# First product of an MLP: the 64-row remainder of its contraction as pairs of 64-row matmuls

## The chip, the cores and the metric

The kernel runs on one core of a Trainium2 chip. The metric is the device time of one execution in microseconds; the time before is the median of three executions.

## What is computed

Eight batches of 4224 rows of 192 columns pass through a dynamic convolution, a two-dimensional Fourier mixing and an MLP:

```
w = softmax(weight_gen)                      # 8 heads, 7 taps
x = causal convolution of x_in with w, per head
X = real(fft(fft(x, axis=1), axis=2))
u = x + X
un = (u - mean(u)) / sqrt(var(u) + 1e-6)
ch = maximum(un @ w_ch1, 0.0) @ w_ch2        # 192 -> 768 -> 192
out = u + ch
```

## The kernel before, in words

A batch's 4224 rows are laid out as 33 rows on each of 128 partitions. Four of those rows make a group (a tile of 128 partitions, 4 rows, 192 columns); a batch has eight groups of four and one of a single row, so there are 72 groups, 64 of them full. Per batch the stages are: `conv` (taps and sums, mostly on VectorE and GpSimd, with the first Fourier factor on TensorE, result through DRAM), `transform` (second factor, TensorE and ScalarE), `mix` (last factor and the addition to u), `norm` and `mlp`. Each stage is a Python generator. `run` (from L617) advances, of all the generators, the one whose due time is earliest; the due times are set at the end (from L685). So the program text interleaves the stages of neighbouring batches. The tile framework then orders the instructions of every engine by its own simulated times, and adds the semaphores; the order that an engine gets is not that of the text.

`norm` (L504) computes statistics on ScalarE, scales u to `un` (f32) and splits it in two fp16 parts: `hl` holds the rounded part (ScalarE, L538) and the rest (`lo`, on GpSimd, for the first few groups on VectorE, L540 and L542). Per row that is 384 columns: 192 rounded and 192 rest. One DMA transpose (L545, SP's queue) turns them into `ht`: per row three blocks of 128 partitions. Block 0 holds columns 0 to 127 rounded, block 2 the rest of those columns, block 1 the remaining 64 columns: rounded on partitions 0–63 and their rest on partitions 64–127.

`mlp(n)` (L550) runs the first product of group n and the second product of group n−1 side by side. The weights are split the same way: `w1h0`, `w1l0` (128 rows of W1, rounded and rest) and `w1h1`, `w1l1` (the last 64 rows, held twice, on partitions 0–63 and 64–127). For each of the six chunks c of 128 hidden columns, five matmuls (L570) add up in one PSUM bank `ph` (three buffers), all of 128 rows and 4 × 128 = 512 columns:

```
terms = ((w1h0, 0), (w1l0, 0), (w1h0, 2), (w1h1, 1), (w1l1, 1))
for i, (wt, blk) in enumerate(terms):
    nc.tensor.matmul(ph[:, 0:T], lhsT=wt[:, cs_], rhs=ht[:, 0:T, blk], ...)
```

ScalarE then takes the ReLU out of the bank to fp16 (`hh`, L580; f32 in the first nine groups, L576), and VectorE the rest of it (`hlo`, L581). The second product (L597) takes hh and hlo of one row and one chunk as the stationary operand and 192 columns of W2 as the moving one: three matmuls per row and chunk (one f32 matmul in the first nine groups), added up in `po` (two banks, two rows each). When all chunks are through, VectorE adds both banks to u (L604) and SP's queue writes it out (L607).

In the sections below, a matmul of 64 rows is called a half.

Of the kernel before, what the change touches and what calls it, by code (L numbers as in the profile page):

```python
# [19 lines left out]
P = 128  # L20
# [18 lines left out]
F32_GROUPS = 9  # L39
# [48 lines left out]
def tile_dynconv_fnet_mlp(  # L88
# [12 lines left out]
    nc = tc.nc  # L101
    B, D = x.shape[0], x.shape[3]
# [3 lines left out]
    NH = DFF // P  # L106
    w1 = w1.bitcast(I32).rearrange("r (c t) -> r c t", t=2)
    w2 = w2.bitcast(I32).rearrange("r (c t) -> r c t", t=2)
    NG = 9

    cpool = ctx.enter_context(tc.tile_pool(name="cpool", bufs=1))
    sb = ctx.enter_context(tc.tile_pool(name="sb", bufs=2))
# [3 lines left out]
    def pst(tag, bufs, shape, dt, name):  # L116
        return ps.tile(shape, dt, tag=tag, name=name, bufs=bufs)
# [14 lines left out]
    w1h0 = cpool.tile([P, DFF], F16, name="w1h0")  # L132
    w1l0 = cpool.tile([P, DFF], F16, name="w1l0")
    w1h1 = cpool.tile([P, DFF], F16, name="w1h1")
    w1l1 = cpool.tile([P, DFF], F16, name="w1l1")
    w2h = cpool.tile([P, NH, D], F16, name="w2h")
    w2l = cpool.tile([P, NH, D], F16, name="w2l")
    w2f = cpool.tile([P, NH, D], F32, name="w2f")
    isc = cpool.tile([P, 1], F32, name="isc")
# [364 lines left out]
    def norm(b, g):  # L504

        T = min(4, N2 - 4 * g)
        u = uv = us[b, g]
        st = sb.tile([P, 4, 2], F32, tag="st", name=f"st_{b}_{g}", bufs=2)
        rs = sb.tile([P, 3, 4], F32, tag="rs", name=f"rs_{b}_{g}", bufs=2)
        junk = sb.tile([P, D], F16, tag="junk", name=f"junk_{b}_{g}", bufs=2)  # L510
        un = sb.tile([P, 4, D], F32, tag="un", name=f"un_{b}_{g}", bufs=1)
        quick = NG * b + g < QUICK or (b == 1 and g < 2)
        if quick:
            bn = sb.tile([P, 4, 6], F32, tag="bn", name=f"bn_{b}_{g}", bufs=2)
            for t in range(T):
                nc.vector.bn_stats(out=bn[:, t, :], in_=uv[:, t, :])
                last_bn[b, g] = nc.vector.bn_aggr(out=st[:, t, :], in_=bn[:, t, :])
            nc.scalar.activation(rs[:, 0, 0:T], st[:, 0:T, 1], AF.Sqrt, bias=eps_t)
            neg = -1.0
        else:  # L520
            for t in range(T):
                nc.scalar.activation(junk, uv[:, t, :], AF.Identity, accum_out=st[:, t, 0:1])  # L522
            neg = -1.0 / D
            nc.scalar.mul(rs[:, 2, 0:T], st[:, 0:T, 0], neg)
            for t in range(T):
                nc.scalar.activation(junk, uv[:, t, :], AF.Square, bias=rs[:, 2, t:t + 1],  # L526
                                     accum_out=st[:, t, 1:2])
            nc.scalar.activation(rs[:, 0, 0:T], st[:, 0:T, 1], AF.Sqrt, bias=eps_t, scale=1.0 / D)
        nc.vector.reciprocal(out=rs[:, 0, 0:T], in_=rs[:, 0, 0:T])
        for t in range(T):  # L530
            nc.vector.tensor_scalar(out=rs[:, 1, t:t + 1], in0=st[:, t, 0:1], scalar1=rs[:, 0, t:t + 1],  # L531
                                    scalar2=neg, op0=ALU.mult, op1=ALU.mult)
        for t in range(T):
            nc.scalar.activation(un[:, t, :], uv[:, t, :], AF.Identity,  # L534
                                 bias=rs[:, 1, t:t + 1], scale=rs[:, 0, t:t + 1])
        yield 0.5
        hl = sb.tile([P, 4, 2 * D], F16, tag="hl", name=f"hl_{b}_{g}", bufs=2)
        nc.scalar.copy(hl[:, 0:T, 0:D], un[:, 0:T, :])  # L538
        lo_eng = nc.vector if quick else nc.gpsimd
        lo_eng.tensor_tensor(out=hl[:, 0:T, 2 * P:3 * P], in0=un[:, 0:T, 0:P],  # L540
                                in1=hl[:, 0:T, 0:P], op=ALU.subtract)
        last_lo[NG * b + g] = lo_eng.tensor_tensor(out=hl[:, 0:T, D:2 * P], in0=un[:, 0:T, P:D],  # L542
                                in1=hl[:, 0:T, P:D], op=ALU.subtract)
        ht = sb.tile([P, 4, 3, P], F16, tag="ht", name=f"ht_{b}_{g}", bufs=3)
        nc.sync.dma_start(ht[:, 0:T].rearrange("p t q m -> p (t q) m"),  # L545
                          hl[:, 0:T, :].rearrange("p t d -> p (t d)"), transpose=True)
        state[b, g] = (us.pop((b, g)), ht)
        yield 2.0

    def mlp(n):  # L550

        now = last = None
        if n < total:
            b, g = divmod(n, NG)
            T = min(4, N2 - 4 * g)
            u, ht = state.pop((b, g))
            now = (b, g, u, [], [])
        if n - 1 in pending:
            last = pending.pop(n - 1)
            lb, lg, lu, hh, hlo = last  # L560
            LT = min(4, N2 - 4 * lg)
            LJ = (LT + 1) // 2
            po = [pst("po", 2, [P, 2, D], F32, f"po_{lb}_{lg}_{jj}") for jj in range(LJ)]
        for c in range(NH):
            if now:
                ph = pst("ph", 3, [P, 4, P], F32, f"ph_{b}_{g}_{c}")
                cs_ = slice(c * P, (c + 1) * P)
                terms = ((w1h0, 0), (w1l0, 0), (w1h0, 2), (w1h1, 1), (w1l1, 1))
                for i, (wt, blk) in enumerate(terms):
                    last_ph[n] = nc.tensor.matmul(ph[:, 0:T], lhsT=wt[:, cs_], rhs=ht[:, 0:T, blk],  # L570
                                                  start=(i == 0), stop=(i == len(terms) - 1))
                    if i < len(terms) - 1:
                        yield (c + 0.1 * (i + 1)) / NH
                if NG * b + g < F32_GROUPS:
                    a, l = sb.tile([P, 4, P], F32, tag="hh", name=f"hh_{b}_{g}_{c}", bufs=10), None
                    nc.scalar.activation(a[:, 0:T], ph[:, 0:T], AF.Relu)  # L576
                else:
                    al = sb.tile([P, 2, 4, P], F16, tag="hh", name=f"hh_{b}_{g}_{c}", bufs=10)
                    a, l = al[:, 0], al[:, 1]
                    nc.scalar.activation(a[:, 0:T], ph[:, 0:T], AF.Relu)  # L580
                    nc.vector.scalar_tensor_tensor(out=l[:, 0:T], in0=ph[:, 0:T], scalar=0.0,  # L581
                                                   in1=a[:, 0:T], op0=ALU.max, op1=ALU.subtract)
                now[3].append(a)
                now[4].append(l)
                yield (c + 0.5) / NH
            if last:
                s, half = divmod(c, NH // 2)
                for c2 in (2 * half, 2 * half + 1):
                    for jj in range(LJ):
                        t = 2 * jj + s  # L590
                        if t >= LT:
                            continue
                        terms = ((hh[c2], w2f),) if NG * lb + lg < F32_GROUPS else (
                            (hh[c2], w2h), (hh[c2], w2l), (hlo[c2], w2h))
                        nt = len(terms)
                        for i, (hx, wx) in enumerate(terms):
                            nc.tensor.matmul(po[jj][:, s, :], lhsT=hx[:, t], rhs=wx[:, c2, :],  # L597
                                             start=(c2 == 0 and i == 0), stop=(c2 == NH - 1 and i == nt - 1))
                            yield (c + 0.5 + 0.25 * (c2 % 2) + 0.25 * (nt * jj + i + 1) / (nt * LJ)) / NH
                if c == NH - 1:  # L600
                    for jj in range(LJ):
                        m = min(2, LT - 2 * jj)
                        lt = lu[:, 2 * jj:2 * jj + m]
                        nc.vector.scalar_tensor_tensor(out=lt, in0=po[jj][:, 0:m],  # L604
                                                       scalar=scales[0][:, 1:2] if NG * lb + lg < F32_GROUPS else isc, in1=lt,
                                                       op0=ALU.mult, op1=ALU.add)
                    nc.sync.dma_start(out[lb, :, 4 * lg:4 * lg + LT, :], lu[:, 0:LT])  # L607
        yield 1.0
        if now:
            pending[n] = now  # L610
# [30 lines left out]
    last_word, last_split, last_lo, last_bn, last_ph, scales = [], [], {}, {}, {}, []  # L641
# [17 lines left out]
    for g in range(QUICK):  # L659
        add(0.0, 1.0, behind((last_word if g else last_split)[-1].ins, mix(0, g)))  # L660
        run()
        add(0.0, 1.0, norm(0, g))
        run()
        queue(last_bn[0, g].ins, (prep_w2, g))
# [74 lines left out]
```

## Time and profile before

| what | value |
|---|---|
| median of three executions | 1191.4 us (1191.09 to 1192.69) |
| the profiled execution's own time | 1194.52 us |
| its span in the trace | 1192.7 us |
| mean granted TensorE clock | 0.963 |
| TensorE busy with matmuls | 1095.0 us |
| VectorE, GpSimd, ScalarE busy | 1027.1, 867.8, 779.2 us |
| first-product matmuls of 512 columns | 1920 |
| second-product matmuls, fp16 | 4158 |

In the profile, PE is TensorE's matmuls and PEld its weight loads; DVE is VectorE, ACT ScalarE, POOL GpSimd, SP the queue that issues the DMAs. A row of a timeline has the start, the time that the merged instructions took, the engine and line, the operation, the tiles written and read, the shape and the count. Matmuls are pipelined: a recorded one overlaps the next, so what one costs in a row of many is the distance of the starts, not its duration.

### The profile page before, as it was taken

The numbers are of one execution on the slowest core, as the hardware profiler recorded it, in microseconds if no ns is written. First come the engines' busy times: TensorE is split into PE (matmuls) and PEld (weight loads), VectorE is DVE, ScalarE is ACT, GpSimd is POOL, SyncE is SP. The second block draws the span as 40 slices with busy tenths as digits, with TensorE's granted clock in tenths as the row PEclk, the third lists the DMA queues.
The fourth block names the chain that finished last, engine by engine and source line by source line (L and its number), as shares of the span: only waits on it lengthen the run. The fifth ranks groups of instructions, "written<-read, shape, count | busy, mean of one in ns | idle before, by whom it ended". The sixth has DMA issues, their size and how long they took to land. (4 is left out here: it accounts for less than half of the span.)

```text
span 1192.7 us, 23723 instructions
## 1 busy us (share of the span) xinstructions
PE 1095.0 (92%) x8382; PEld 827.0 (69%) x8382; DVE 1027.1 (86%) x2041; ACT 779.2 (65%) x2353; POOL 867.8 (73%) x686
## 2 busy tenths in 40 slices
PE   4775599899899979998999999899989999999998
PEld 2444377678667857687677777678667876877677
DVE  7999998789999999899999999799998997367533
ACT  1015695254597598757895789657885799589732
POOL 3869579839896999699978999599958997002100
PEclk9896599999999989999999999899999999999999
DMA  8235233731348144733474247413543124412311
GB/s 305 84 98 163 40 60 109 192 89 47 99 127 206 50 123 102 191 87 88 112 198 110 61 114 208 125 48 110 147 121 92 54 58 102 111 45 71 75 50 44
DMA packets 156504, 128.73 MB, mean 108 GB/s; under 512 B 108571, under 2 KB 133088, under 8 KB 156384
## 3 DMA queue, kind: packets, MB, share of 16 engines
q1 hardware_dynamic: 156384, 127.21, 39.4%
q8 instruction: 66, 1.08, 0.4%
q14 instruction: 54, 0.44, 0.1%
HBM read 61.46 MB, written 39.37 MB: 85 GB/s over the span
## 5 line engine op out<-in xcount | busy, mean ns | idle before, releaser
L399 POOL TENSOR_TENSOR u<-u,pr 128x768 f32<-128x768 f32 (+1 forms) x395 | 655.3, 1679 | 69.5 <-DVE pr L390 62.6
L570 PE MATMUL ph<-ht,w1h 128*128 128x512 f16 (+1 forms) x1296 | 401.2, 366 | 20.1 <-DMA ht<-hl 8.8
L597 PE MATMUL po<-w2h,hh 128*128 128x192 f16 x2772 | 395.1, 247 | 6.4 <-DVE u L604 6.0
L597 PEld LDWEIGHTS <-hh 128*128 128x128 f16 x4158 | 355.0, 98 | 65.6 <-issue 7.8
L390 DVE TENSOR_TENSOR pr<-x_sb,wp 128x768 f32<-128x768 f32 (+1 forms) x420 | 358.0, 878 | 21.3 <-POOL u L399 16.8
L597 PE MATMUL po<-w2l,hh 128*128 128x192 f16 x1386 | 337.1, 247 | 0.0
L581 DVE SCALAR_TENSOR_TENSOR hh<-ph,hh 128x512 f16<-128x512 f32 (+1 forms) x378 | 238.7, 640 | 98.1 <-ACT hh L580 96.8
L570 PE MATMUL ph<-ht,w1l 128*128 128x512 f16 (+1 forms) x864 | 312.6, 365 | 0.0
L580 ACT ACTIVATE hh<-ph 128x512 f16<-128x512 f32 (+1 forms) x378 | 207.8, 555 | 136.6 <-PE ph L570 135.7
L540 POOL TENSOR_TENSOR hl<-un,hl 128x512 f16<-128x512 f32 (+1 forms) x67 | 71.9, 1073 | 175.3 <-ACT hl L538 129.4
L570 PEld LDWEIGHTS <-w1h 128*128 128x128 f16 x1296 | 127.2, 100 | 101.6 <-issue 6.1
L534 ACT ACTIVATE un<-u,rs 128x192 f32<-128x192 f32 x264 | 125.6, 537 | 19.8 <-DVE rs L531 12.2
L570 PEld LDWEIGHTS <-w1l 128*128 128x128 f16 x864 | 85.3, 99 | 73.2 <-issue 22.1
L526 ACT ACTIVATE junk<-u,rs 128x192 f16<-128x192 f32 x244 | 110.4, 453 | 3.5
L522 ACT ACTIVATE junk<-u 128x192 f16<-128x192 f32 x244 | 87.8, 360 | 16.6 <-DVE u L496 12.1
L486 PE MATMUL eo<-cs_sb,pq 97*128 97x97 f32 x544 | 79.8, 282 | 17.8 <-DVE u L496 13.3
L486 PEld LDWEIGHTS eo<-cs_sb,pq 97*128 97x128 f32 x544 | 73.8, 198 | 24.4 <-issue 13.1
L461 ACT COPY pq<-pp 97x204 f32<-97x204 f32 (+1 forms) x96 | 46.4, 483 | 60.3 <-PE pp L457 59.4
L597 PE MATMUL po<-w2f,hh 128*128 128x192 f32 x396 | 74.3, 337 | 3.5 <-DVE u L604 3.5
L597 PEld LDWEIGHTS po<-w2f,hh 128*128 128x128 f32 x396 | 68.3, 197 | 9.2 <-DVE u L604 5.2
L604 DVE SCALAR_TENSOR_TENSOR u<-po,isc,u 128x384 f32<-128x384 f32 (+1 forms) x119 | 68.0, 597 | 7.7 <-PE po L597 7.2
L395 PE MATMUL pa<-pr,ident 128*128 128x384 f32 x140 | 54.6, 540 | 20.5 <-DVE pr L390 17.8
(101 smaller groups left out, 1309.7 us busy)
## 6 DMA issues: line engine op xcount, KB each, us to landing
out_dram<-u SPq DMA_DIRECT2D x64, 384.0 KB
x_sb<-in_x_dram SPq DMA_DIRECT2D x48, 384.0 KB
g<-g_d SPq DMA_DIRECT2D x40, 336.0 KB
x_sb<-in_x_dram SPq DMA_DIRECT2D x8, 864.0 KB
g_d<-gt SPq DMA_DIRECT2D x32, 195.0 KB
g_d<-gt SPq DMA_DIRECT2D x32, 189.0 KB
w<-in_weight_gen_dram SPq DMA_DIRECT2D x6, 924.0 KB
x_sb<-in_x_dram SPq DMA_DIRECT2D x8, 672.0 KB
```

Of the source, the lines that this page charges most:

```text
L390: last_product[b] = nc.vector.tensor_tensor(out=dst, in0=rows, in1=wk, op=ALU.mult)
L399: adder.tensor_tensor(out=u, in0=u, in1=pr, op=ALU.add)
L486: nc.tensor.matmul(eo[:, e, j, :], lhsT=pq[0:DH, e, r, r:r + P], rhs=cs_sb[:, e, :], start=True, stop=True)
L522: nc.scalar.activation(junk, uv[:, t, :], AF.Identity, accum_out=st[:, t, 0:1])
L526: nc.scalar.activation(junk, uv[:, t, :], AF.Square, bias=rs[:, 2, t:t + 1], accum_out=st[:, t, 1:2])
L534: nc.scalar.activation(un[:, t, :], uv[:, t, :], AF.Identity, bias=rs[:, 1, t:t + 1], scale=rs[:, 0, t:t + 1])
L540: lo_eng.tensor_tensor(out=hl[:, 0:T, 2 * P:3 * P], in0=un[:, 0:T, 0:P], in1=hl[:, 0:T, 0:P], op=ALU.subtract)
L570: last_ph[n] = nc.tensor.matmul(ph[:, 0:T], lhsT=wt[:, cs_], rhs=ht[:, 0:T, blk], start=(i == 0), stop=(i == len(terms) - 1))
L580: nc.scalar.activation(a[:, 0:T], ph[:, 0:T], AF.Relu)
L581: nc.vector.scalar_tensor_tensor(out=l[:, 0:T], in0=ph[:, 0:T], scalar=0.0, in1=a[:, 0:T], op0=ALU.max, op1=ALU.subtract)
L597: nc.tensor.matmul(po[jj][:, s, :], lhsT=hx[:, t], rhs=wx[:, c2, :], start=(c2 == 0 and i == 0), stop=(c2 == NH - 1 and i == nt - 1))
L604: nc.vector.scalar_tensor_tensor(out=lt, in0=po[jj][:, 0:m], scalar=scales[0][:, 1:2] if NG * lb + lg < F32_GROUPS else isc, in1=lt, op0=A ...
```

## The change

For full groups (T = 4) the first product is cut differently. Chunks are taken in pairs, and a bank `ph` no longer holds four rows of one chunk, but two rows of both chunks of the pair: the pair's first bank holds rows 0 and 1, its second one rows 2 and 3. The terms on the first 128 columns (L595) are now six matmuls of 256 columns per bank. The 64-column remainders (L605) are matmuls of 64 rows: `norm` lays the transposed remainder out so that partitions 0–63 of blocks 8 to 11 belong to rows 0 and 1 and partitions 64–127 to rows 2 and 3, and each term is issued twice, once on each half of the partitions, each into its own bank. Three terms × two chunks × two halves make twelve per pair. ReLU and its rest (`keep`) stay one instruction per bank at the old shape. In the second product the index of `hh` changes accordingly, and the loop runs row by row through all chunks, so that the first two rows are finished and added to u halfway (L634). In `norm` the rounding copy becomes two (L547, L548), of 128 and 64 columns per row.

```diff
-        nc.scalar.copy(hl[:, 0:T, 0:D], un[:, 0:T, :])
...
+        if T == 4:
+            flat = hl.rearrange("p t d -> p (t d)")
+            hi0, lo0 = [flat[:, o:o + 4 * P].rearrange("p (t d) -> p t d", t=4) for o in (0, 4 * P)]
+            hi1, lo1 = [flat[:, o:o + 2 * P].rearrange("p (a s d) -> p s a d", a=2, s=2) for o in (8 * P, 10 * P)]
+            un0, un1 = un[:, :, 0:P], un[:, :, P:D].rearrange("p (s a) d -> p s a d", s=2)
...
+        nc.scalar.copy(hi0, un0)
+        nc.scalar.copy(hi1, un1)
+        lo_eng.tensor_tensor(out=lo0, in0=un0, in1=hi0, op=ALU.subtract)
+        last_lo[NG * b + g] = lo_eng.tensor_tensor(out=lo1, in0=un1, in1=hi1, op=ALU.subtract)
...
+            if now and T == 4:
+                j = c % 2
                 ph = pst("ph", 3, [P, 4, P], F32, f"ph_{b}_{g}_{c}")
+                ph2 = [ph] if j == 0 else [ph2[0], ph]
+                pair = (c - j, c - j + 1)
+                for c1 in pair:
+                    co = 2 * (c1 % 2)
+                    for i, (wt, blk) in enumerate(((w1h0, 0), (w1l0, 0), (w1h0, 4))):
+                        last_ph[n] = nc.tensor.matmul(ph[:, co:co + 2], lhsT=wt[:, c1 * P:(c1 + 1) * P],
+                                                      rhs=ht[:, blk + 2 * j:blk + 2 * j + 2],
+                                                      start=(co == 0 and i == 0), stop=False)
+                        yield (c + 0.06 * (3 * (c1 % 2) + i + 1)) / NH
+                if j == 1:
+                    for c1 in pair:
+                        co = 2 * (c1 % 2)
+                        for i, (wt, blk) in enumerate(((w1h1, 8), (w1l1, 8), (w1h1, 10))):
+                            for q in range(2):
+                                h = slice(64 * q, 64 * q + 64)
+                                last_ph[n] = nc.tensor.matmul(ph2[q][:, co:co + 2], lhsT=wt[h, c1 * P:(c1 + 1) * P],
+                                                              rhs=ht[h, blk:blk + 2], start=False,
+                                                              stop=(c1 == c and i == 2))
+                    for q in range(2):
+                        keep(ph2[q], 4)
+                yield (c + 0.5) / NH
...
+                for k in range(per * c, per * (c + 1)):
+                    t, c2 = divmod(k, NH)
+                    i2, t2 = (2 * (c2 // 2) + t // 2, 2 * (c2 % 2) + t % 2) if LT == 4 else (c2, t)
```

What this makes of the order on TensorE, at two places. A name such as ph_5_0_2_10033 is the bank of batch 5, group 0, chunk 2 and a running number; in the change, the bank of an even chunk is the first of its pair and gets the halves on partitions 0–63, that of the odd chunk behind it is the second and gets those on partitions 64–127.

TensorE before, batch 5, group 0, chunk 2, from its second matmul to the second products behind it:

```order
L570 LDWEIGHTS w1l0_82
L570 MATMUL ph_5_0_2_10033<-ht_5_0_9665,w1l0_82 128x512
L570 LDWEIGHTS w1h0_81
L570 MATMUL ph_5_0_2_10033<-ht_5_0_9665,w1h0_81 128x512
L570 LDWEIGHTS w1h1_83
L570 MATMUL ph_5_0_2_10033<-ht_5_0_9665,w1h1_83 128x512
L570 LDWEIGHTS w1l1_84
L570 MATMUL ph_5_0_2_10033<-ht_5_0_9665,w1l1_84 128x512
L597 LDWEIGHTS hh_4_8_5_9946
L597 MATMUL po_4_8_0_9970<-w2h_85,hh_4_8_5_9946 128x192
```

TensorE with the change, the same group, from the fifth of the six halves of the pair's first bank (chunk 2) to the first full matmul of its second (chunk 3):

```order
L605 LDWEIGHTS w1l1_84
L605 MATMUL ph_5_0_2_11768<-ht_5_0_11362,w1l1_84 128x256
L605 LDWEIGHTS w1h1_83
L605 MATMUL ph_5_0_2_11768<-ht_5_0_11362,w1h1_83 128x256
L418 MATMUL pg_6_4_11868<-sm_6_4_11865,f1_sb_67 128x192 x2
L629 LDWEIGHTS hh_4_8_5_11674
L629 MATMUL po_4_8_0_11697<-w2h_85,hh_4_8_5_11674 128x192
L595 LDWEIGHTS w1h0_81
L595 MATMUL ph_5_0_3_11783<-ht_5_0_11362,w1h0_81 128x256
```

All six halves of the first bank have moved up behind its full matmuls; the six on the other partitions stand behind the full matmuls of chunk 3, with other work between.

TensorE with the change, batch 2, group 5, chunks 0 and 1, where the halves begin:

```order
L595 MATMUL ph_2_5_1_6300<-ht_2_5_5830,w1h0_81 128x256
L605 LDWEIGHTS w1h1_83
L605 MATMUL ph_2_5_0_6244<-ht_2_5_5830,w1h1_83 128x256
L605 LDWEIGHTS w1h1_83
L605 MATMUL ph_2_5_1_6300<-ht_2_5_5830,w1h1_83 128x256
L605 LDWEIGHTS w1l1_84
L605 MATMUL ph_2_5_0_6244<-ht_2_5_5830,w1l1_84 128x256
L605 LDWEIGHTS w1l1_84
L605 MATMUL ph_2_5_1_6300<-ht_2_5_5830,w1l1_84 128x256
```

Here the halves alternate between the two banks, as the code is written. Over the whole program there are 2304 full matmuls (L595) and 2304 halves (L605) of 256 columns; a half has one on the other partitions as its neighbour in 433 disjoint pairs, and 1438 stand without a partner. Runs of halves begin 347 times and end 347 times.

More of the change, by code (lines that the diff above doesn't have):

```diff
@@ L537, in norm @@
         hl = sb.tile([P, 4, 2 * D], F16, tag="hl", name=f"hl_{b}_{g}", bufs=2)
-        nc.scalar.copy(hl[:, 0:T, 0:D], un[:, 0:T, :])
         lo_eng = nc.vector if quick else nc.gpsimd
[L540 to L546, printed above, removed]
+        if T == 4:
[3 more added lines that the diff above has]
+            un0, un1 = un[:, :, 0:P], un[:, :, P:D].rearrange("p (s a) d -> p s a d", s=2)
+        else:
+            hi0, hi1, lo1, lo0 = hl[:, 0:T, 0:P], hl[:, 0:T, P:D], hl[:, 0:T, D:2 * P], hl[:, 0:T, 2 * P:3 * P]
+            un0, un1 = un[:, 0:T, 0:P], un[:, 0:T, P:D]
+        nc.scalar.copy(hi0, un0)
+        nc.scalar.copy(hi1, un1)
+        lo_eng.tensor_tensor(out=lo0, in0=un0, in1=hi0, op=ALU.subtract)
+        last_lo[NG * b + g] = lo_eng.tensor_tensor(out=lo1, in0=un1, in1=hi1, op=ALU.subtract)
+        ht = sb.tile([P, 12, P], F16, tag="ht", name=f"ht_{b}_{g}", bufs=3)
+        nc.sync.dma_start(ht[:, 0:3 * T], hl[:, 0:T, :].rearrange("p t d -> p (t d)"), transpose=True)
         state[b, g] = (us.pop((b, g)), ht)
@@ L563, in mlp, with keep @@
             po = [pst("po", 2, [P, 2, D], F32, f"po_{lb}_{lg}_{jj}") for jj in range(LJ)]
+        def keep(ph, w):
+            nm = f"hh_{b}_{g}_{len(now[3])}"
+            if NG * b + g < F32_GROUPS:
+                a, l = sb.tile([P, 4, P], F32, tag="hh", name=nm, bufs=10), None
+                nc.scalar.activation(a[:, 0:w], ph[:, 0:w], AF.Relu)
+            else:
+                al = sb.tile([P, 2, 4, P], F16, tag="hh", name=nm, bufs=10)
+                a, l = al[:, 0], al[:, 1]
+                nc.scalar.activation(a[:, 0:w], ph[:, 0:w], AF.Relu)
+                nc.vector.scalar_tensor_tensor(out=l[:, 0:w], in0=ph[:, 0:w], scalar=0.0,
+                                               in1=a[:, 0:w], op0=ALU.max, op1=ALU.subtract)
+            now[3].append(a)
+            now[4].append(l)
@@ L564, in mlp @@
         for c in range(NH):
-            if now:
+            cs_ = slice(c * P, (c + 1) * P)
+            if now and T == 4:
+                j = c % 2
                 ph = pst("ph", 3, [P, 4, P], F32, f"ph_{b}_{g}_{c}")
-                cs_ = slice(c * P, (c + 1) * P)
+                ph2 = [ph] if j == 0 else [ph2[0], ph]
[19 more added lines that the diff above has]
+                yield (c + 0.5) / NH
+            elif now:
+                ph = pst("ph", 3, [P, 4, P], F32, f"ph_{b}_{g}_{c}")
@@ L568, in mlp @@
                 terms = ((w1h0, 0), (w1l0, 0), (w1h0, 2), (w1h1, 1), (w1l1, 1))
                 for i, (wt, blk) in enumerate(terms):
-                    last_ph[n] = nc.tensor.matmul(ph[:, 0:T], lhsT=wt[:, cs_], rhs=ht[:, 0:T, blk],
+                    last_ph[n] = nc.tensor.matmul(ph[:, 0:T], lhsT=wt[:, cs_], rhs=ht[:, blk:blk + T],
                                                   start=(i == 0), stop=(i == len(terms) - 1))
@@ L573, in mlp @@
                         yield (c + 0.1 * (i + 1)) / NH
[L574 to L582, printed above, removed]
@@ L583, in mlp @@
-                now[3].append(a)
-                now[4].append(l)
+                keep(ph, T)
                 yield (c + 0.5) / NH
             if last:
[L587 to L599, printed above, removed]
@@ L600, in mlp @@
-                if c == NH - 1:
[L601 to L606, printed above, removed]
+                f32 = NG * lb + lg < F32_GROUPS
@@ new lines, in mlp @@
+                per = LT
+                for k in range(per * c, per * (c + 1)):
+                    t, c2 = divmod(k, NH)
+                    i2, t2 = (2 * (c2 // 2) + t // 2, 2 * (c2 % 2) + t % 2) if LT == 4 else (c2, t)
+                    terms = ((hh[i2], w2f),) if f32 else ((hh[i2], w2h), (hh[i2], w2l), (hlo[i2], w2h))
+                    for i, (hx, wx) in enumerate(terms):
+                        nc.tensor.matmul(po[t // 2][:, t % 2, :], lhsT=hx[:, t2], rhs=wx[:, c2, :],
+                                         start=(c2 == 0 and i == 0), stop=(c2 == NH - 1 and i == len(terms) - 1))
+                        yield (c + 0.5 + 0.5 * (k - per * c + (i + 1) / len(terms)) / per) / NH
+                    if c2 == NH - 1 and (t % 2 == 1 or t == LT - 1):
+                        lt = lu[:, t - t % 2:t + 1]
+                        nc.vector.scalar_tensor_tensor(out=lt, in0=po[t // 2][:, 0:t % 2 + 1],
+                                                       scalar=scales[0][:, 1:2] if f32 else isc, in1=lt,
+                                                       op0=ALU.mult, op1=ALU.add)
```

## The prediction

> **What bounds the kernel now.** I read the busy shares first, then the busy time by stage, then the chain of waits near the end, then the timeline of TensorE alone. The busy shares:
>
> ```profile
> PE 1095.0 (92%) x8382; PEld 827.0 (69%) x8382; DVE 1027.1 (86%) x2041; ACT 779.2 (65%) x2353; POOL 867.8 (73%) x686
> ```
>
> The windows (a busy time and a count for PE, PEld, DVE, ACT, POOL, then clock, DMA share, GB/s):
>
> ```profile
> 0.00:150.00 150.00, 95.44 (x354) 61.08 (x355) 136.81 (x264) 46.77 (x132) 101.70 (x84) 0.81 0.44 137
> 150.00:1000.00 850.00, 810.30 (x6381) 621.22 (x6380) 795.85 (x1565) 615.08 (x1875) 743.46 (x573) 0.98 0.42 112
> 1000.00:1180.00 180.00, 180.00 (x1539) 136.00 (x1537) 90.21 (x204) 115.74 (x342) 22.61 (x30) 1.00 0.27 69
> ```
>
> After 1000 us TensorE is the only bound: it is never idle there and everyone else has half the time free or more. From 150 to 1000 us it is idle for 850 − 810.3 = 39.7 us in all, with VectorE close behind (795.85). So work added to TensorE after 150 us goes nearly one for one into the time; only those 39.7 us can swallow some of it. Work taken from TensorE pays fully only in the last stage.
>
> What a matmul costs is read from the chain of waits near the end, where they follow each other without a gap:
>
> ```profile
> 1142.55 3.24 PE ph L570 x15
> 1145.79 2.97 PE po L597 x36
> 1148.76 1.08 PE ph L570 x5
> ```
>
> Fifteen first-product matmuls of 512 columns take 3.24 us: 0.216 each. The 192-column ones of the second product take 2.97/36 = 0.0825. In the last, one-row group the matmuls have 128 columns (timeline of TensorE):
>
> ```profile
> 1179.63 0.22 PE L570 MATMUL ph<-ht,w1h 128*128 128x128 f16 x1
> 1179.69 0.22 PE L570 MATMUL ph<-ht,w1l 128*128 128x128 f16 x1
> 1179.75 0.28 PE L570 MATMUL ph<-ht,w1h 128*128 128x128 f16 x2
> 1179.86 0.22 PE L570 MATMUL ph<-ht,w1l 128*128 128x128 f16 x1
> 1179.91 0.22 PE L570 MATMUL ph<-ht,w1h 128*128 128x128 f16 x1
> ```
>
> From the first start to the sixth: (1179.91 − 1179.63)/5 = 0.056. Between 0.056 at 128 and 0.216 at 512 a straight line gives 0.0827 at 192, as measured, so I take it for 256 columns, which the trace doesn't have: 0.056 + 0.160/3 = 0.1093 us, an estimate from these rows. Each of these matmuls has its own weight load; loads hide behind the matmul ahead, even at 0.056.
>
> **The first product's matmuls.** There are 64 groups of four rows. Before: 64 × 30 = 1920 matmuls of 512 columns, 1920 × 0.216 = 414.7 us. Now each group has 36 matmuls on all 128 rows and 36 on 64 rows ("halves"), all of 256 columns. The full ones: 2304 × 0.1093 = 251.8 us, whatever the order. The halves cost what their order makes of them. A half on partitions 0–63 writes the pair's first bank, one on 64–127 the second. Two that stand next to each other share neither rows of the array, nor partitions, nor a bank, and I count them as one: 0.1093 us for both. The trace has no two matmuls at once; the least start distance in the rows above is one stream, so the other bound is 0.2186 for two. I take the lower, since they share nothing that the rows show to be busy, and keep the other.
>
> The code writes the halves alternating, but the program isn't in that order: the scheduler has put six halves of one bank behind that bank's full matmuls, and those of the other bank behind other work. Counted over the whole program, of 2304 halves 433 × 2 stand beside a partner and 1438 stand alone. So halves take (433 + 1438) × 0.1093 = 204.5 us. First product: 251.8 + 204.5 = 456.3, **41.6 us more than before**, because a lone half keeps the whole array for 64 rows' worth of work. Had all 1152 pairs stayed together it would be 251.8 + 125.9 = 377.7, that is 37.0 less.
>
> **The switches of the array's shape.** TensorE now changes between 128-row and 64-row matmuls 347 times each way, 694 in all. Before, almost nothing changes shape, but four changes lie in one place where nothing else was waited for long: the matmuls of one column (L181) and of one row (L184) among second products. Timeline of TensorE in two windows:
>
> ```profile
> 241.88 1.14 PE L597 MATMUL po<-w2f,hh 128*128 128x192 f32 x6
> 242.94 0.38 PE L181 MATMUL mr_w<-ident,m_w 128*1 128x128 f32 x2
> 243.25 0.59 PE L597 MATMUL po<-w2f,hh 128*128 128x192 f32 x2
> ```
>
> ```profile
> 246.12 0.65 PE L597 MATMUL po<-w2f,hh 128*128 128x192 f32 x3
> 246.70 0.38 PE L184 MATMUL me_w<-m_w,ones 1*128 1x1 f32 x2
> 247.01 0.39 PE L570 MATMUL ph<-ht,w1h 128*128 128x512 f16 x1
> 247.24 0.38 PE L570 MATMUL ph<-ht,w1l 128*128 128x512 f16 x1
> 247.45 0.38 PE L570 MATMUL ph<-ht,w1h 128*128 128x512 f16 x1
> ```
>
> A matmul that follows normally starts 0.16 before the recorded end of the one ahead: 247.24 against 247.01 + 0.39 = 247.40. At each of the four changes the overlap is only 0.07 or 0.08: 242.94 against 243.02, 243.25 against 243.32, 246.70 against 246.77, 247.01 against 247.08. So each change holds the array up for 0.09 us. The first fp16 matmul after one takes 247.24 − 247.01 = 0.23 instead of 0.216, since its weights weren't loaded ahead: 0.01 more. I take 0.10 per change: 694 × 0.10 = **69.4 us**. Bounds: 0, if a 64-row shape (not in this trace) needs no such wait; and 0.19, if the reload shows as it does for fp32, where two second products after the change take 0.59 against 0.33 + 0.16 = 0.49: 694 × 0.19 = 131.9.
>
> The Trainium skill, page "TensorEngine Tiling (Array Packing)", section "Key Properties", says that changing the tiling mode drains the TensorE and that changing only the tile does not. The four rows agree with its first half (0.09 each). It gives no price; with 0 in its place the sum would be 69.4 less. Its second half no run here shows yet; the rival in which alternating halves pay too is priced below from rows.
>
> The page "TensorE: Matmul & The Clock Gate", section "Packing small matmuls — row/col tiling", puts the distance between two matmuls on different rows at about 4 ns; that would be 433 × 0.004 = 1.7 us beside my sum. No row here shows it.
>
> **The other edits.** Evacuation keeps six ReLUs and six subtractions per group at the same shapes (L580, L581), so nothing. Where halves are paired, a bank is drained only after both are full, so two ReLUs queue on ScalarE at once and both subtractions stand behind them; TensorE goes on with second products of the group before, and a third bank is free. The second product now finishes two rows midway and releases its bank then; TensorE's waits in 150:1000 show what that can help:
>
> ```profile
> PE po L597 <- DVE u L604: 9.1, 9, 1.8
> PE ph L570 <- DMA ht<-hl: 8.8, 3, 4.1
> PE pp L457 <- DMA g<-g_d: 7.6, 3, 3.9
> PE ph L570 <- DVE hh L581: 6.4, 7, 1.7
> ```
>
> ScalarE's rounding copy in norm is cut in two. By the two forms of the old one,
>
> ```profile
> L538 ACT CAST hl<-un 128x768 f16<-128x768 f32 x64 | 52.9, 827 | 0.7 <-DMA ht<-hl 0.5
> L538 ACT CAST hl<-un 128x192 f16<-128x192 f32 x8 | 2.8, 349 | 3.4 <-DMA ht<-hl 3.3
> ```
>
> a column costs (827 − 349)/576 = 0.83 ns and the rest 190 ns, which is paid twice: 64 × 0.19 = 12.2 us on an engine that is 65% busy and works a group ahead. Its reader is the DMA transpose behind it on SP's queue, for which TensorE waits 8.8 us in all. I cost it at nothing; uncovered, 12.2. VectorE and GpSimd do the same subtractions on other strides: nothing, with no row to say more. SP's queue carries the same DMAs in size and number.
>
> **The sum.** TensorE gets 41.6 + 69.4 = 111.0 us more. Of the 39.7 us idle I let half be swallowed, 20: the waits for u and hh (15.5) go when TensorE is later than VectorE, and part of the two DMA waits, whose chains now run ahead. What is late next is TensorE itself. The profiled execution: 1194.5 + 111.0 − 20 = 1285.5; it lies 3.1 above the median of the runs (1191.4), so **1282 us**. With all or none of the idle swallowed: 1262 to 1302.
>
> **Rivals.**
> - *Neighbouring halves don't overlap.* For it: no two matmuls overlap in any row here. Against: they share no rows or bank. 433 × 0.1093 = 47.3 more: 1330.
> - *The 64-row shape changes free of charge.* For it: the rows are of other shapes. Against: two different shapes, each entered and left, gave 0.09 every time. 69.4 less: 1213.
> - *Changes cost 0.19.* For it: the fp32 row above. Against: the fp16 one. 62.5 more: 1345.
> - *Alternating halves pay for the change too.* 807 times a half follows one on the other rows: 807 × 0.09 = 72.6, and the overlap's 47.3 is lost as well: 1402. Against: nothing in the rows.
> - *Faster, by the overlap.* If the array could bring every half together with its partner and changes cost nothing, the first product would be 37.0 shorter; all of it on the path gives 1154. It decides at (251.8 + 251.8 − 414.7)/0.1093 = 813 overlapped pairs without any cost for changes; the order has 433, and with 69.4 us of changes even all 1152 don't suffice. This would need halves that start out of their order, which no row shows: every matmul in the rows above starts after the one ahead.
>
> That the change doesn't do what it says is half of the forecast: its pairs are mostly not pairs in the program.
>
> **How the numbers follow.** Forecast 0.55, no overlap 0.18, free changes 0.10, dear changes 0.10, alternation pays 0.04, faster 0.03. Leaving out the free changes, the alternation and the faster case (0.17) the range runs from 1240 (below the forecast's own 1262, for changes that cost somewhat less) to 1350, which holds the no-overlap and the dear-change cases. A measurement of this kernel can tell about 0.2% from no change. Faster by more than that 0.03, within it 0.01, slower 0.96.
>
> **What would show it.** Right: TensorE busy about 94% of the span (1095 + 111 of 1284), VectorE's and GpSimd's shares lower; lone halves starting 0.11 apart; the first matmul after each change starting about 0.07 instead of 0.16 before the end ahead; in alternating runs two starts close together and the next two 0.11 later; about 0.86 us for a run of six lone halves with the changes at its two ends. Wrong: full overlap at 0.07 or less per half everywhere, no late start at changes, or new idle time on TensorE before 1000 us.

## The result, and the profile after

Four executions of the changed kernel have a median of 1296.87 us (1290.37 to 1301.91), four of the kernel before 1191.87. The ratio is 1.0869, 95% interval 1.0821 to 1.0917: slower by 8.7%. The forecast was 1282 us with a range of 1240 to 1350. The profiled execution took 1301.91 us, its span is 1300.1.

The busy shares after:

```profile
PE 1213.1 (93%) x11070; PEld 988.8 (76%) x11070; DVE 1031.9 (79%) x2041; ACT 791.1 (61%) x2425; POOL 868.9 (67%) x686
```

TensorE's busy time has grown by 118.1 us, that of VectorE, ScalarE and GpSimd by 12 or less. Its idle time has shrunk from 1192.7 − 1095.0 = 97.7 to 1300.1 − 1213.1 = 87.0. The difference, 118.1 − 10.7 = 107.4 us, is the whole growth of the span. By stage (windows of the changed kernel, columns as in the prediction):

```profile
150.00:1000.00 850.00, 823.32 (x7680) 682.27 (x7680) 730.61 (x1401) 555.27 (x1702) 686.19 (x528) 0.98 0.40 106
1000.00:1180.00 180.00, 178.47 (x1828) 149.97 (x1823) 113.16 (x266) 130.02 (x424) 71.45 (x62) 1.00 0.28 69
1180.00:1300.00 120.00, 117.18 (x1205) 96.23 (x1202) 51.65 (x112) 58.33 (x165) 9.62 (x12) 1.00 0.20 49
```

In the long middle VectorE fell from 796 us busy to 731. Over the whole span its work is the same (1031.9 us against 1027.1), stretched over a longer time, while TensorE is idle in this stage for 850 − 823.3 = 26.7 us only. Its waits in this stage for the addition to u, for the subtraction that frees a bank, and for the DMA of ht:

```profile
PE po L629 <- DVE u L634: 7.4, 3, 3.9
PE ph L595 <- DVE hh L580: 6.3, 5, 2.4
PE ph L595 <- DMA ht<-hl: 0.5, 1, 0.5
```

A run of lone halves in the timeline of TensorE:

```profile
903.39 0.27 PE L595 MATMUL ph<-ht,w1l 128*128 128x256 f16 x1
903.50 0.27 PE L595 MATMUL ph<-ht,w1h 128*128 128x256 f16 x1
903.70 0.28 PE L605 MATMUL ph<-ht,w1h 64*128 64x256 f16 x1
903.82 0.27 PE L605 MATMUL ph<-ht,w1l 64*128 64x256 f16 x1
903.93 0.38 PE L605 MATMUL ph<-ht,w1h 64*128 64x256 f16 x2
904.15 0.27 PE L605 MATMUL ph<-ht,w1l 64*128 64x256 f16 x1
904.26 0.27 PE L605 MATMUL ph<-ht,w1h 64*128 64x256 f16 x1
904.46 0.34 PE L629 MATMUL po<-w2h,hh 128*128 128x192 f16 x2
```

Full matmuls follow each other at 0.11, and lone halves too: half the rows cost as much as all of them. At the two changes of shape the next start comes 0.20 later (903.50 to 903.70, 904.26 to 904.46) instead of 0.11, and the matmul behind the first change takes 0.12 (903.70 to 903.82). The six halves with their two changes take 904.46 − 903.50 − 0.11 = 0.85 us; the prediction said about 0.86. And where the halves stand in pairs:

```profile
1125.63 0.27 PE L595 MATMUL ph<-ht,w1h 128*128 128x256 f16 x1
1125.84 0.28 PE L605 MATMUL ph<-ht,w1h 64*128 64x256 f16 x2
1125.96 0.27 PE L605 MATMUL ph<-ht,w1l 64*128 64x256 f16 x2
1126.07 0.38 PE L605 MATMUL ph<-ht,w1h 64*128 64x256 f16 x4
1126.28 0.27 PE L605 MATMUL ph<-ht,w1l 64*128 64x256 f16 x2
1126.49 0.33 PE L457 MATMUL pp<-te_sb,g 102*97 102x102 f32 x1
```

Two matmuls together take 0.27 or 0.28, no longer than one alone: they start within 0.01 of each other, and the next two come 0.11 later. From the first pair's start to the next other matmul, 1126.49 − 1125.84 = 0.65 us hold five pairs and a change of 0.09: 0.112 for a pair, or 0.110 if the 0.01 behind the change is taken out as well. So the overlap is real, and changing from one half of the partitions to the other costs nothing that these rows show. The Trainium skill's page "TensorE: Matmul & The Clock Gate" (section "Packing small matmuls — row/col tiling") says that such matmuls run at the same time, and the Trainium skill's page "TensorEngine Tiling (Array Packing)" (section "Key Properties") that only a change of mode, not of the tile, drains the array; the trace agrees with both.

### The profile page after: what moved, and what is told of

It reads as the page before. It is cut to its first block, busy times and chain, and to the rows that moved or that the text cites. A ratio compares the mean times of both kernels' runs of the same rounds, so it can differ in the third digit from the quotient of the medians.

```text
span 1300.1 us, 29071 instructions
## 1 busy us (share of the span) xinstructions
PE 1213.1 (93%) x11070; PEld 988.8 (76%) x11070; DVE 1031.9 (79%) x2041; ACT 791.1 (61%) x2425; POOL 868.9 (67%) x686
## 4 chain that ended last, share of the span: by engine, by line
PE 62%; DVE 19%; DMA 7%; ACT 4%; issue 4%; POOL 3%; SPq 0%; DVEq 0%; POOLq 0%; ACTq 0%
PE po L629 23%; PE ph L595 15%; PE ph L605 14%; DVE pr L390 7%; PE pp L457 5%; PE eo L486 3%; POOL u L399 2%; PE pg L418 2%; DMA out_dram<-u 2%; DMA g<-g_d 2%; DVE hh L580 2%; DMA g_d<-gt 1%; PE pa L395 1%; DVE u L390 1%; DVE u L634 1%
## 5 line engine op out<-in xcount | busy, mean ns | idle before, releaser
L629 PE MATMUL po<-w2h,hh 128*128 128x192 f16 x2772 | 415.7, 248 | 4.4 <-DVE u L634 4.1
L629 PEld LDWEIGHTS <-hh 128*128 128x128 f16 x4158 | 343.5, 99 | 52.8 <-issue 44.4
L595 PE MATMUL ph<-ht,w1h 128*128 128x256 f16 x1536 | 325.1, 277 | 12.9 <-DVE hh L580 7.1
L605 PE MATMUL ph<-ht,w1h 64*128 64x256 f16 x1536 | 264.7, 275 | 0.0
L595 PE MATMUL ph<-ht,w1l 128*128 128x256 f16 x768 | 212.4, 277 | 0.0
L605 PEld LDWEIGHTS <-w1h 64*128 64x128 f16 x1536 | 120.0, 94 | 83.2 <-issue 67.7
L595 PEld LDWEIGHTS <-w1h 128*128 128x128 f16 x1536 | 153.2, 100 | 29.6 <-issue 13.4
L605 PE MATMUL ph<-ht,w1l 64*128 64x256 f16 x768 | 174.2, 272 | 0.0
L486 PE MATMUL eo<-cs_sb,pq 97*128 97x97 f32 x544 | 88.7, 287 | 15.6 <-DVE u L496 15.6
L595 PEld LDWEIGHTS <-w1l 128*128 128x128 f16 x768 | 76.2, 99 | 22.0 <-issue 14.6
L634 DVE SCALAR_TENSOR_TENSOR u<-po,isc,u 128x384 f32<-128x384 f32 (+1 forms) x119 | 71.0, 597 | 23.1 <-PE po L629 22.7
```

The source lines that it names most:

```text
L486: nc.tensor.matmul(eo[:, e, j, :], lhsT=pq[0:DH, e, r, r:r + P], rhs=cs_sb[:, e, :], start=True, stop=True)
L595: last_ph[n] = nc.tensor.matmul(ph[:, co:co + 2], lhsT=wt[:, c1 * P:(c1 + 1) * P], rhs=ht[:, blk + 2 * j:blk + 2 * j + 2], start=(co == 0 ...
L605: last_ph[n] = nc.tensor.matmul(ph2[q][:, co:co + 2], lhsT=wt[h, c1 * P:(c1 + 1) * P], rhs=ht[h, blk:blk + 2], start=False, stop=(c1 == c ...
L629: nc.tensor.matmul(po[t // 2][:, t % 2, :], lhsT=hx[:, t2], rhs=wx[:, c2, :], start=(c2 == 0 and i == 0), stop=(c2 == NH - 1 and i == len( ...
L634: nc.vector.scalar_tensor_tensor(out=lt, in0=po[t // 2][:, 0:t % 2 + 1], scalar=scales[0][:, 1:2] if f32 else isc, in1=lt, op0=ALU.mult, o ...
```

## The experiments

The theory to be tested: TensorE is the path, a lone half costs 0.109 us, a pair 0.112, a change of shape 0.105 (with the weights behind it), and the scheduler parts the pairs because a third bank is all it has. Rival A: changes of shape are hidden, the lone halves are the whole loss. Rival B: the other edits (banks held longer, row-by-row second product, two copies) lose the time. Rival C, after the first runs: waits for banks lose it. Each run's ratio is to the kernel before, with its 95% interval.

**All pairs together.** Each half is ordered behind the one that the code writes before it:

```diff
+                                with tc.issue_after(last_ph[n].ins):
                                     last_ph[n] = nc.tensor.matmul(ph2[q][:, co:co + 2], ...)
```

> The change with every half ordered behind the one that the code writes before it, so that 1147 pairs stand together and 398 changes of shape are left (the change: 433 and 694). Theory (lone halves at 0.109 us and changes at 0.105 make the loss): first product 251.8 + 1147 x 0.112 + 10 x 0.109 + 398 x 0.105 = 423 us against 529 in the change and 415 before, so about 1200 us. Rival A (only the lone halves cost, changes of shape are hidden): 382 us, 33 less than before, about 1165. Rival B (the loss lies in the other edits: banks held longer, second product by rows, two copies): it stays near 1290.

1364.22 us, 1.144 (1.1398 to 1.1482): slower than the change, and at the number of none of the three theories. Its busy shares, and then who made TensorE wait:

```profile
PE 1163.1 (85%) x11070; PEld 965.5 (71%) x11070; DVE 1029.3 (76%) x2041; ACT 787.5 (58%) x2425; POOL 871.4 (64%) x686
```

```profile
PE ph L595 <- DVE hh L580: 64.6, 37, 6.0
PE po L630 <- ACT hh L579: 27.3, 28, 3.8
```

TensorE's busy time did fall against the change, by 50 us (although at a lower granted clock, 0.927 against 0.966), but its idle time rose by 111 us, to 1361.4 − 1163.1 = 198.3. A pair holds two of the three banks until its last half. Both are then drained one behind the other, ReLU and subtraction each, and meanwhile the next pair has one bank. This kernel's TensorE waits 64.6 us for that subtraction, and 27.3 us with its second products for the ReLU that they read. In the change TensorE's waits for VectorE in the MLP are these:

```profile
PE po L629 <- DVE u L634: 8.0, 4, 3.9
PE ph L595 <- DVE hh L580: 7.1, 6, 2.4
```

The theory's price of the work was not the whole story: keeping pairs together has a price in banks. The last three runs test this.

**The rest of the change alone.** Norm's two copies and the second product row by row; the first product as before, on 512 columns (cut from the edit against the kernel before; the two copies are not shown):

```diff
-                s, half = divmod(c, NH // 2)
-                for c2 in (2 * half, 2 * half + 1):
-                    for jj in range(LJ):
-                        t = 2 * jj + s
...
+                for k in range(per * c, per * (c + 1)):
+                    t, c2 = divmod(k, NH)
+                    i2, t2 = c2, t
```

> The rest of the change alone: norm's two copies and the second product row by row, with the first product as before (five matmuls of 512 columns per bank). Theory: nothing, 1192 us within 5. Rival B: a large part of the 105 us, 1220 or more.

1185.24 us, 0.9942 (0.9925 to 0.9958): 7 us faster than before. Rival B falls for these two edits: they gain a little. Its third part, banks held longer, is not in this kernel; the waits answer it, with 7.1 us for a bank in the change against 6.4 before.

**Changes of shape alone.** In the kernel before, the fifth matmul of each chunk uses 64 rows:

```diff
+                    h = slice(0, 64) if i == 4 and T == 4 else slice(0, P)
-                    last_ph[n] = nc.tensor.matmul(ph[:, 0:T], lhsT=wt[:, cs_], rhs=ht[:, 0:T, blk],
+                    last_ph[n] = nc.tensor.matmul(ph[:, 0:T], lhsT=wt[h, cs_], rhs=ht[h, 0:T, blk],
```

> The kernel before, with the last of the five matmuls (w1l1) on partitions 0-63 alone: same number, same columns, 768 changes of shape more. It leaves out the product of the two rest parts. Theory: 768 x 0.105 = 81 us more on TensorE, 10 to 20 of it swallowed by its idle time: 1255 to 1265 us. Rival A: 1192.

1251.97 us, 1.0498 (1.0482 to 1.0513). The same matmuls with the same columns, 768 changes: 59.6 us, 0.078 of the time for each. It is 3 us under the range that the theory gave. Its busy shares:

```profile
PE 1170.1 (94%) x8382; PEld 787.2 (63%) x8382; DVE 1030.9 (82%) x2041; ACT 785.7 (63%) x2353; POOL 866.7 (69%) x686
```

TensorE is busy 1170.1 − 1095.0 = 75.1 us longer, 0.098 for each change (81 us, 0.105 each, were expected), and its idle time shrinks from 97.7 to 1250.4 − 1170.1 = 80.3, so 17.4 us of the work are taken in. In the timeline a change costs what it should:

```profile
1100.17 0.59 PE L571 MATMUL ph<-ht,w1h 128*128 128x512 f16 x2
1100.69 0.39 PE L571 MATMUL ph<-ht,w1l 64*128 64x512 f16 x1
1101.01 0.26 PE L598 MATMUL po<-w2h,hh 128*128 128x192 f16 x1
```

The starts 1100.69 and 1101.01 lie 0.07 before the recorded end ahead (1100.76 and 1101.08) instead of 0.16, so each is 0.09 late. Rival A falls: changes aren't hidden.

**No change of shape.** The change, with each half run over all 128 rows (its sums take in the other two rows' remainders too):

```diff
-                                last_ph[n] = nc.tensor.matmul(ph2[q][:, co:co + 2], lhsT=wt[h, c1 * P:(c1 + 1) * P],
-                                                              rhs=ht[h, blk:blk + 2], start=False,
+                                last_ph[n] = nc.tensor.matmul(ph2[q][:, co:co + 2], lhsT=wt[:, c1 * P:(c1 + 1) * P],
+                                                              rhs=ht[:, blk:blk + 2], start=False,
```

> The change with each half run on all 128 rows: as many matmuls and columns, no change of shape, nothing that can overlap. It adds the remainders of the other two rows to each sum. Theory: first product 4608 x 0.109 = 503 us against 529: about 1271 us. Rival A: 503 against 456, about 1340. Rival B: as the change, 1297.

1278.05 us, 1.0721 (1.0696 to 1.0746). Its busy shares, and those of the rest of the change alone:

```profile
PE 1179.4 (93%) x11070; PEld 1080.2 (85%) x11070; DVE 1023.3 (80%) x2041; ACT 788.6 (62%) x2425; POOL 871.0 (68%) x686
```

```profile
PE 1090.4 (92%) x8382; PEld 821.5 (69%) x8382; DVE 1026.7 (87%) x2041; ACT 785.4 (66%) x2425; POOL 868.3 (73%) x686
```

TensorE's busy time is 1179.4 − 1090.4 = 89.0 us longer; 4608 matmuls of 256 columns at 0.1093 instead of 1920 at 0.216 give 88.9. This is the cleanest check of the pitch that was interpolated. The change is 19 us slower than this kernel although 433 of its pairs overlap: its 694 changes cost more than the overlap saves. The expected number was 1271; it is 7 higher.

**All halves apart.** Each bank's halves directly behind its full matmuls:

```diff
+                for c1 in pair:
+                    co = 2 * (c1 % 2)
+                    for i, (wt, blk) in enumerate(((w1h1, 8), (w1l1, 8), (w1h1, 10))):
+                        h = slice(64 * j, 64 * j + 64)
...
+                            last_ph[n] = nc.tensor.matmul(ph[:, co:co + 2], lhsT=wt[h, c1 * P:(c1 + 1) * P], ...)
```

> The change with the halves of each bank issued directly behind that bank's full matmuls: no pair is left together, 2304 lone halves and 800 changes of shape (the change: 1438 lone, 433 pairs, 694 changes). Theory (lone halves at 0.109, changes at 0.105): 433 x 0.109 + 106 x 0.105 = 58 us over the change, 1355. Rival C (keeping two banks until both are full is what costs, as in the kernel with all pairs together): no bank waits for a second one here, so it would be faster than the change, 1270 or less.

1340.19 us, 1.1238 (1.1208 to 1.1268), 43 over the change. Busy time grows by 1267.4 − 1213.1 = 54.3 against the 58 expected; idle time falls from 87.0 to 1336.8 − 1267.4 = 69.4, so the time grows by less than the work. It is not the waiting for banks that shrinks: TensorE waits 9.9 us for the subtraction that frees one, against 7.1 in the change. The wait for the addition to u (8.0 in the change) is gone, and that for g's DMA fell from 16.4 to 9.1.

```profile
PE 1267.4 (95%) x11070; PEld 1015.0 (76%) x11070; DVE 1029.9 (77%) x2041; ACT 800.0 (60%) x2425; POOL 871.2 (65%) x686
```

Rival C's number for this run, 1270 or less, is missed by 70.

**A fourth bank, by moving the softmax weights to SBUF.** In the kernel before (control) and in the change; to make room in SBUF, both runs also have one buffer less of two small tiles (`sm` and `junk`), which this cut does not show:

```diff
-            wbanks[b] = pst("wp", 1, [P, 512], F32, f"wp_{b}")
+            wbanks[b] = sb.tile([P, 512], F32, tag="wp", name=f"wp_{b}", bufs=1)
-                ph = pst("ph", 3, ...)
+                ph = pst("ph", 4, ...)
```

> The kernel before with the softmax weights in SBUF instead of PSUM and the freed bank as a fourth one for the first product (paid for in SBUF by one buffer less of two small tiles). A control for the next run. Theory: TensorE's work is the same, so 1192 us within 15; VectorE reads the taps from another memory, whose price no run shows.

> The change, with its code for the first product untouched, and the same fourth bank as in the control. The order now has 1058 pairs together, 188 lone halves and 470 changes of shape. Theory (the third bank is what made the scheduler part the halves and what made TensorE wait when they were kept together): first product 251.8 + 1058 x 0.112 + 188 x 0.109 + 470 x 0.105 = 440 us, 25 over the control's 415, less some 7 for the second product by rows: 10 to 30 over the control. Rival C (waits for banks as with all pairs together on three banks): 100 or more over the control.

The control took 1517.66 us, 1.2723 (1.2694 to 1.2751), the change 1547.53, 1.2971 (1.2942 to 1.3). The expectation of the control failed by 325 us, and with it the pair as a test of the theory: the change is 30 us over its control, at the end of the 10 to 30 expected, but TensorE is busy for only 665 of the 850 us of the middle stage in both, so its work is not the path there. Why, the groups show, first of the kernel before, then of the control:

```profile
L399 POOL TENSOR_TENSOR u<-u,pr 128x768 f32<-128x768 f32 x347 | 627.7, 1829 | 59.4 <-DVE pr L390 53.8
L390 DVE TENSOR_TENSOR pr<-x_sb,wp 128x768 f32<-128x768 f32 x372 | 342.6, 946 | 13.5 <-POOL u L399 9.0 <-DMA x_sb<-in_x_dram 2.2 <-PE pa L395 1.1
```

```profile
L399 POOL TENSOR_TENSOR u<-u,pr 128x768 f32<-128x768 f32 x347 | 775.7, 2251 | 111.6 <-DVE pr L390 93.7 <-DVE u L390 5.9 <-DVE u L399 3.5
L390 DVE TENSOR_TENSOR pr<-x_sb,wp 128x768 f32<-128x768 f32 x372 | 606.1, 1654 | 9.3 <-POOL u L399 7.1 <-PE pa L395 2.0
```

VectorE's product of a tap takes 1654 ns instead of 946, GpSimd's sum 2251 instead of 1829. One thing the pair does show is the order: with a fourth bank and the first product's code untouched, the scheduler keeps 1058 pairs together where on three banks it kept 433.

**The second product row by row alone.** The loop above, norm untouched.

> The kernel before with the second product row by row alone (the first two rows finished and added to u midway), norm untouched. Theory: this is what made the rest of the change 7 us faster, so 1185 us as there; if the two copies did it, 1192.

1184.85 us, 0.9934 (0.9912 to 0.9957), the same as the rest of the change alone. So the row-by-row second product gains the 7 us, and the two copies cost nothing that can be told. TensorE's wait for the addition to u is gone; before, and in this kernel:

```profile
PE po L597 <- DVE u L604: 9.5, 10, 1.8
PE po L594 <- DVE u L599: 0.5, 2, 0.4
```

This is the fastest version that came up, and it has no halves.

**A fourth bank from the second product.** Its two banks become one, and the taps stay in PSUM (the other users of these banks move along, in all three runs); on the kernel with the row-by-row second product (control), on the change, and on the kernel with all pairs together:

```diff
-            po = [pst("po", 2, [P, 2, D], F32, f"po_{lb}_{lg}_{jj}") for jj in range(LJ)]
+            po = {}
...
+                    if t // 2 not in po:
+                        po[t // 2] = pst("po", 1, [P, 2, D], F32, f"po_{lb}_{lg}_{t // 2}")
-                ph = pst("ph", 3, ...)
+                ph = pst("ph", 4, ...)
```

> The kernel before with the second product row by row and with one bank for it instead of two, the freed bank going to the first product as a fourth one (taps stay in PSUM). A control for the next two. Theory: the single second-product bank makes TensorE wait up to 0.6 us at each of 128 hand-overs unless other matmuls stand there: between 1185 and 1230 us.

> The change, its first product untouched, with the same four banks. The order now has 885 pairs together, 534 lone halves and 580 changes of shape (the change on three banks: 433, 1438, 694). Theory (the want of a bank made the scheduler part the halves): 251.8 + 885 x 0.112 + 534 x 0.109 + 580 x 0.105 = 470 us for the first product, 55 over the control and 59 under the change: 40 to 60 over the control. Rival C (the loss is in waits for banks, whatever the order): 100 or more over the control.

> The change with the halves in the order of the code, as in the kernel with all pairs together, now on four banks: 1121 pairs, 62 lone halves, 504 changes of shape. Theory: first product 437 us, 22 over the control, if the fourth bank ends the waits that cost 170 us on three: 10 to 50 over the control. Rival C: 100 or more over the control.

| kernel on four banks | us | ratio, interval | over the control |
|---|---|---|---|
| control | 1216.5 | 1.0202 (1.0184 to 1.022) | |
| the change | 1256.87 | 1.0542 (1.0526 to 1.0558) | 40.4 (40 to 60 expected) |
| all pairs together | 1245.47 | 1.044 (1.042 to 1.046) | 29.0 (10 to 50 expected) |

All three lie within what was expected, the change at the lower edge. The fourth bank, paid for with a slower second product, makes the change 40 us faster and the kernel with all pairs together 119 us faster. In the change the scheduler now keeps 885 pairs together instead of 433, and TensorE's busy time falls from 1213.1 to 1157.3:

```profile
PE 1157.3 (92%) x11070; PEld 961.0 (77%) x11070; DVE 1023.0 (82%) x2041; ACT 782.8 (62%) x2425; POOL 871.7 (69%) x686
```

Its wait for the subtraction that frees a bank does not fall (10.5 us, 7.1 on three banks). So the gain is in the work, by more pairs and fewer changes, and not in waiting. The busy shares of the kernel with all pairs together, and its wait for a bank:

```profile
PE 1127.4 (90%) x11070; PEld 948.3 (76%) x11070; DVE 1026.3 (82%) x2041; ACT 785.9 (63%) x2425; POOL 870.4 (70%) x686
```

```profile
PE ph L595 <- DVE hh L580: 11.5, 15, 1.8
```

64.6 us of waiting for the subtraction have become 11.5, and against its control the busy time differs by 1127.4 − 1098.0 = 29.4 us, which accounts for the 29.0 between the medians (the spans of the two profiled executions differ by 33.7). The control's row:

```profile
PE 1098.0 (91%) x8382; PEld 827.8 (68%) x8382; DVE 1025.6 (85%) x2041; ACT 769.8 (63%) x2353; POOL 869.2 (72%) x686
```

Rival C is right about all pairs on three banks and wrong about the change itself: there TensorE waits 7.1 us for a bank, hardly more than before (6.4), because the scheduler had given up the pairs instead.

## Why the prediction was right, step by step

- *TensorE's time is the time.* Shown: 118.1 us more busy, 10.7 less idle, 107.4 more span. One reading beside it is wrong: after 1000 us not everyone else has half the time free, as ScalarE is busy for 115.74 of the 180 us, 64%. The sum doesn't rest on it, since TensorE is never idle there.
- *Matmuls of 256 columns at 0.1093.* Shown by the kernel on all rows: 89.0 against 88.9 us.
- *Lone halves cost a whole stream, pairs one for two.* Shown in the timeline and by taking all pairs apart (54.3 us more busy, 58 expected).
- *694 changes at 0.10.* The mechanism is right, and the rows of L181 and L184 gave the price: in the changed kernel, starts at a change are about 0.09 late, and the first fp16 matmul behind it is 0.01 longer. The kernel with changes alone shows it by itself: 0.098 us of TensorE's time for each.
- *The sum of the first product's work*, 111.0 us, stands against 118.1 that all of TensorE's work grew by. At 0.112 for a pair and 0.105 for a change, the prices that the experiments go by, 433 × 0.003 + 694 × 0.005 = 4.8 us of the difference would be explained; the rest was not separated.
- *20 us swallowed.* This term was mis-sized. From 150 to 1000 us the idle time went from 39.7 to 850 − 823.32 = 26.7, so 13 were swallowed there; before and behind this stage the idle time grew by 2, which leaves 10.7 in all. They came from another wait than the text took them from. It counted on the waits for u and hh, 15.5 us in this stage, which in the change are still 13.7; what went is the wait for the DMA of ht, from 8.8 to 0.5. That the term came out as near as it did is in part luck. Over the whole span, the wait for the addition to u went as forecast in the kernel without halves (9.5 to 0.5), but in the change it is still 8.0, in four waits. Both terms erred to the same side: 118.1 − 111.0 = 7.1 and 20 − 10.7 = 9.3 make the 16.4 us between 1285.5, forecast for the profiled execution, and its 1301.9.
- *The other edits at nothing.* They gain 7 us, all by the row-by-row second product. The text named the wait, and counted it within the 20.
- *Banks held longer at nothing.* The text counted on second products and a third bank to cover the draining of a pair. For the change this came out (7.1 us of waiting, 6.4 before), but in part because most pairs had been parted; with the pairs kept together on three banks it does not hold (64.6).
- *The rivals.* No overlap, free changes, changes at 0.19 (0.20 from start to start, stream and change together), paying alternation and the faster case are refuted by the timelines above.

What the prediction did not see: why the pairs were apart. It took the order as given; the two sets of runs with a fourth bank show that three banks for a pair that holds two make the scheduler part most of them (433 kept on three banks, 885 and 1058 on four), and that forcing them together on three banks costs 67 us more than parting them.

## What to carry to other kernels

Two 64-row matmuls overlap only if they stand next to each other in TensorE's order, so count neighbours in the built order, not in the code; a lone one costs as much as a full matmul of as many columns, and every entry to and exit from the 64-row shape about 0.1 us. Here even all pairs together would save 37 us of streaming, and the 398 changes that were left with them cost 42 at 0.105: no gain is left when the array goes over to 64 rows for six pairs at a time. A pair needs two accumulators at once, and with too few banks either the scheduler gives the pairs up or TensorE waits for the draining.

## What the runs showed of the hardware that was not expected

Moving the taps of the convolution's products from PSUM to SBUF made VectorE's product 1654 ns instead of 946 and, at the same time, GpSimd's sum 2251 instead of 1829; the kernel as a whole became 27% slower, with two small tiles short of a buffer as well. The slowdown is not SBUF's own speed. In the control with the taps in SBUF, this is what VectorE and GpSimd do from 1304.47 us on (VectorE's products and GpSimd's sums; the other rows are left out):

```profile
1304.47 0.95 DVE L390 TENSOR_TENSOR u<-x_sb,wp 128x768 f32<-128x768 f32 x1
1305.33 0.95 DVE L390 TENSOR_TENSOR pr<-x_sb,wp 128x768 f32<-128x768 f32 x1
1306.36 6.78 POOL L399 TENSOR_TENSOR u<-u,pr 128x768 f32<-128x768 f32 x3 [3.21 <-DVE pr L390]
1307.07 1.92 DVE L390 TENSOR_TENSOR pr<-x_sb,wp 128x768 f32<-128x768 f32 x1
```

GpSimd is idle for 3.21 us up to 1306.36, and the two products in that time take 0.95 each, as with the taps in PSUM. The product beside GpSimd's sums takes 1.92. Of the 429 products of this size in that trace, 58 meet no GpSimd instruction, and their mean is 948 ns. So the two engines slow each other when VectorE's product has both inputs in SBUF. The Trainium skill's page "SBUF — State Buffer", section "SBUF: two separate sides", names a port pair for this, which a VectorE operation with two SBUF inputs and a GpSimd operation that reads SBUF both need: the one that starts first holds it, and the other waits. The rows agree, with both engines slower only beside each other; the ports themselves no row shows.
